# A skip weight added by two identity products on TensorE instead of an addition on VectorE, with the hand-written order rewritten

## The chip, the cores and the metric

One core of one Trainium2 chip runs the whole kernel as one program. The metric is the device time of one execution in microseconds, median of the runs shown. Engine names below are those of the profile: PE (TensorE matmul), PEld (its weight loads), DVE (VectorE), ACT (ScalarE), POOL (GpSimd), SP (SyncE, which here only issues DMAs).

## The reference, cut to what matters

```python
def A(q, k, v, shift_k, ssm_k, ssm_D):            # q, k, v: 2048 x 512 bf16
    k_shift = sum(k_pad[:, t:t+S] * shift_k[:, 3-t] for t in range(4))
    kv = k_shift * v
    y = long_convolution(kv, ssm_k)                # by FFT over 4096, one filter per channel
    y = y + kv * ssm_D                             # D: one number per channel
    return q * y

x = A_q
x = x + A(layernorm(x), A_k, A_v, ...)
x = x + mlp(layernorm(layernorm(x)))               # 512 -> 1376 (gelu) -> 512
x = x + A(layernorm(x), A_k, A_v, ...)
x = x + mlp(layernorm(layernorm(x)))
```

`kv * D` is the long convolution's tap at lag 0: adding D to the first tap of each channel's filter gives the same sum. That is how the kernel does it. Since `A` multiplies its filter result by its own argument alone, the filter result is computed once and used by both layers.

## The kernel before, in words

The first 100 us or so compute the long convolution as a two-step Fourier transform by matmuls, for the filter and for kv. From 104.5 us on, eight rounds of the MLP (four groups of 512 tokens, twice) run with TensorE as the bound.

Everything in the first part is a named piece in a plan. `plan.add` gives a piece its name, its possible engines, and its function; a long string, `ORDER`, lists the pieces as `name.engine`, in the order in which they are written into the program. Each engine runs its own pieces strictly in that order, and a piece that waits holds all that stand behind it on its engine. `P` in the string is PE with the number of one of four PSUM buffers; `A`, `D`, `G`, `S` are ACT, DVE, POOL, SP. Most PE pieces have a copy out of PSUM, with an `e` at the end of the name, on ACT or DVE (helper `mm_evac`; the copy is L237 on ACT, L239 on DVE).

The pieces that the change and the prediction touch:

- `lk0`..`lk3`, `lh1`, `lh113`, `lv0`, `lv1`, `lsT`: loads of k, of k's rows for the shift, of v, and of the short filter `sT`. `lK00`..`lK11` load the long filter into `Kd`, as packets of 128 bytes. All go through SP (L301, L374).
- `sF` (POOL, L382) casts `sT`; `dg0`..`dg2` (L435) build diagonal matrices DG from it by four small multiplications each.
- `kT0`..`kT3` (PE, L441) transpose k; `kv10` and its like (PE, L524) do the short filter on three of four channel blocks by 32 matmuls each; `kvm10` and its like (DVE, L530) multiply by v. All `kv` pieces need `dg` and most `kTe`.
- `kg0`, `kg1`, `ka1`, ... `kgm` (POOL, L455, L457, L462, L466): the short filter of the fourth channel block, as long element-wise operations one behind the other.
- `s00`, `s01`, `s02`: the layernorm of the first 512 tokens. `s00` is the statistics (on ACT L487 to L490; on DVE L259, L263, L268), `s01` the power on POOL (L271, L495 to L500), `s02` the scaling (on ACT L508; on DVE L276, four TENSOR_SCALAR).
- `U0S0` and its like (PE, L325): first transform step of kv, 12 pieces of four matmuls for three blocks. `KS00`..`KS71` (PE, L400): the same for the filter, 16 pieces; they read `Kd`. `K20`..`K215` (PE, L413): the filter's second step, 16 pieces, which need all `KS`.
- `kd0`, `kd4` (L393): D is added to the filter's first taps. `Kd[:, s, 0]` holds the first tap of each of 128 channels' rows, 64 columns a piece, with a step of 128 bytes; `Dz` is a 128x128 matrix with D at the same places and zeros elsewhere, made by POOL at the start. `kd0` must be done before `KS0x` to `KS3x`, `kd4` before `KS4x` to `KS7x`.

Of the kernel before, what the change touches and what calls it, by code (L numbers as in the profile page):

```python
# [11 lines left out]
ALU = mybir.AluOpType  # L12
# [3 lines left out]


ORDER = """
lSK.S lk1.S lsT.S lk3.S lk0.S lk2.S bSK.P0 lh1.S bSKe.A lh113.S lx0.S kT1.P1 lv0.S sF.G lv1.S dg0.D dg2.D
kT1e.A lK00.S kT3.P2 dg1.D lK01.S kT0.P3 kT3e.A kT2.P0 kT0e.A kg0.G kT2e.D s00.A kv10.P1 kv21.P2 kvm10.D kg1.G  # L20
U1S0.P30 kv11.P0 U1S0e.A kvm21.D U1S1.P1 kvm11.D kv00.P3 U1S1e.A s01.G lK10.S kv01.P2 kvm00.D ka1.G s02.A
U0S0.P01 kvm01.D U1S3.P1 lK11.S kv20.P3 U1S3e.D U0S0e.A kd0.D U0S3.P2 kvm20.D KS11.P1 U0S3e.A KS21.P0 kg2.G
lX.S KS11e.D KS10.P3 KS21e.A KS00.P2 KS10e.A U2S0.P02 KS00e.D KS30.P1 U2S0e.A U2S3.P3 KS30e.D U0S2.P2 U2S3e.A
KS20.P0 lH.S lW.S U2S1.P1 U0S2e.A KS20e.D lM.S KS31.P3 ka2.G lx1.S U2S1e.A KS01.P2 kd4.D KS50.P0 KS31e.A
KS01e.D KS70.P1 KS70e.A KS41.P3 KS50e.D KS61.P2 KS41e.A KS40.P1 KS61e.D KS60.P0 KS40e.A KS51.P3 kg3.G KS60e.D
KS71.P2 KS51e.A U1S2.P1 KS71e.A U2S2.P0 U1S2e.D U0S1.P3 U2S2e.A K211.P2 U0S1e.D K29.P1 K211e.A K210.P0 K29e.D
K28.P3 K210e.A K214.P2 ka3.G K28e.A K24.P1 K214e.D K21.P0 K24e.A K215.P3 sa2.S K21e.D sb2.S K212.P2 K215e.A
K20.P1 K212e.D lb0.S K23.P0 K20e.A lb1.S K22.P3 K23e.D K26.P2 K22e.A kgm.G K25.P1 s10.D K26e.A K27.P0 sb0.S
sa0.S U2T0.P3 K27e.A K213.P2 K25e.A U2T1.P0 K213e.A sa1.S U1T0.P1 U2T0e.D B1.G sb1.S s11.G U2T1e.A sb3.S
U3S0.P22 sa3.S U1T0e.D U1T1.P3 U3S0e.A X20.P00 U1T1e.D U3S2.P1 X20e.A X10.P21 U3S2e.D X21.P32 X10e.A U3S3.P0  # L30
T20.D0 X21e.A U3S1.P1 U0T0.P2 lx.S U3S1e.A T10.D1 X13.P30 U3S3e.A V20.P10 U0T0e.D X13e.A U3T0.S X23.P01 T21.D2
U0T1.P2 V20e.A T13.D0 X00.P32 X23e.A V10.P11 U0T1e.D X00e.A V21.P0 V10e.A T23.D1 X01.P30 V13.P2 V21e.A T00.D2
X02.P11 X01e.A V23.P0 X02e.D V13e.A X03.P32 T01.D0 V23e.A V00.P1 X03e.A T02.D1 X11.P20 V01.P0 V00e.A T03.D2
X12.P31 X11e.A V02.P1 V01e.D X12e.A U3T1.S X30.P22 T11.D0 V02e.A V03.P0 X30e.A T12.D1 X22.P30 V11.P1 V03e.A
T30.D2 X31.P21 X22e.A Z01.S V12.P0 V11e.D X31e.A Z00.S T22.D0 X32.P32 V12e.A V30.P12 X32e.A T31.D1 Z10.S
X33.P20 V22.P0 X33e.A T32.D2 Z03.S V31.P3 V22e.A T33b.D0 V32.P2 Z13.S V31e.A T33a.D1 V33b.P0 V30e.D V32e.A
Z02.S V33a.P3 V33be.D V33ae.A TC0a.P1 TC0b.P2 Z12.S TC0ae.A TD0a.P3 TC1.P0 TC0be.D TD0ae.A Z11.S TD0b.P1
TC1e.D Y00.P2 TD0be.A TC3.P3 w3.S w1.S Y00e.A g00.D w2.S Y01.P1 TC3e.A w4.S TC2.P0 g01.D Y02.P2 h00.D Y01e.A
Y10.P3 h01.D Y02e.A p00.G Y30.P1 TC2e.D Y10e.A p01.G Y12.P2 Y30e.A b00.D g02.D Y22.P3 Y12e.A LT0.P0 Y20.P1
b01.D Y22e.A LT0e.D h02.D Y32.P2 Y20e.A Y32e.D p02.G b02.D  # L40
"""
NA, NB = 32, 64

# [82 lines left out]
def kernel(ctx: ExitStack, tc: tile.TileContext, A_q, A_k, A_v, A_shift_k, A_ssm_k, A_ssm_D,  # L126
                 B_x, B_w1, B_b1, B_w2, B_b2, out):
    nc = tc.nc
    P = 128
    _, S, D = A_q.shape  # L130
# [43 lines left out]
    Kd = place("Kd", [P, P, NB], 64 * K)  # L174
# [8 lines left out]
    IDt = const.tile([P, P], BF16, name="IDt")  # L183
# [12 lines left out]
    B1 = const.tile([P, FT], F32, name="B1")  # L196
# [31 lines left out]
    def view(t, dims, dtype=None):  # L228
        n = int(np.prod(dims))
        v = t[:, :] if dtype is None else t[:, :].bitcast(dtype)  # L230
        names = "abc"[:len(dims)]
        return v[:, 0:n].rearrange("p (%s) -> p %s" % (" ".join(names), " ".join(names)),
                                   **dict(zip(names[1:], dims[1:])))

    def evac(eng, dst, src):
        if eng == "A":
            nc.scalar.activation(dst, src, AF.Copy)  # L237
        else:
            nc.vector.tensor_copy(dst, src)  # L239
# [56 lines left out]
    with tc.tile_pool(name="ps", bufs=1, space=bass.MemoryType.PSUM) as ps:  # L296
        pf = [ps.tile([P, 1024], F32, name=f"p{i}") for i in range(4)]
        plan = _Plan({"ps": 4, "xb": 3, "zt": NZT, "T": NTB})

        def load(name, dst, src, nbytes, deps=(), eng="S", rank=0):  # L300
            return plan.add(name, {eng: 400}, deps, lambda it: nc.sync.dma_start(dst, src), dma=("copy", nbytes), rank=rank)  # L301
# [5 lines left out]
        def mm_evac(name, ns, deps, mms, dims, dst, bf=False, take=(), free_mm=(), edeps=(), rank=0, src=None):  # L307
            src = src or (lambda v: v)
            n = int(np.prod(dims))
            cost = {"A": 85 + 0.82 * n, "D": 50 + (0.53 if bf else 1.06) * n}  # L310
            pe = plan.add(name, {"P": ns}, deps, lambda it: mms(view(pf[it["slot"]["ps"]], dims, BF16 if bf else None)),
                          take=["ps"] + list(take), free=free_mm, rank=rank)
            ev = plan.add(name + "e", cost, [pe] + list(edeps),
                          lambda it: evac(it["eng"], dst(), src(view(pf[pe["slot"]["ps"]], dims, BF16 if bf else None))),
                          free=[(pe, "ps")], rank=rank)
            return pe, ev
# [72 lines left out]
        for c in range(8):  # L389
            if c % (8 // NK) == 0:  # L390
                sl = slice(c * 16, c * 16 + P // NK)
                kd = plan.add(f"kd{c}", {"G": 300, "D": 130}, lK[c * NK // 8], lambda it, sl=sl: (
                    nc.vector if it["eng"] == "D" else nc.gpsimd).tensor_tensor(Kd[:, sl, 0], Kd[:, sl, 0], Dz[:, sl], ALU.add))  # L393
            for g in range(2):
                def mms(o, c=c, g=g):
                    for m in range(8):
                        for e in range(2):
                            rs = slice(64 * g + 32 * e, 64 * g + 32 * e + 32)
                            s0 = 16 * c + 2 * m
                            nc.tensor.matmul(o[:, e, m, :], Kd[rs, s0:s0 + 2, :].rearrange("p s b -> p (s b)"), Ft[rs, 256:320],  # L400
                                             start=True, stop=True)
# [65 lines left out]
        kgm = plan.add("kgm", {"D": 1150, "G": 4200}, kg[-1:] + lv, gmul)  # L467
# [8 lines left out]
        lx0 = load("lx0", lna0, xd[:, 0:GT, :], 2 ** 19)  # L476
        lx1 = load("lx1", x1, xd[:, GT:2 * GT, :], 2 ** 19)
# [32 lines left out]
        _, s2 = first(0, lna0, lx0)  # L510
        s10, _ = first(1, x1, lx1)
        kvp, USp, ZU = [], [], []
        for cc in range(4):
# [4 lines left out]
            for o2 in range(2 if cc < CK else 0):  # L518
                def mms(o, cc=cc, o2=o2):
                    for i in range(8):  # L520
                        for t in range(KS):
# [4 lines left out]
                              lambda it, mms=mms: mms(view(pf[it["slot"]["ps"]], [8, P])), take=["ps"])  # L526
# [9 lines left out]
        lM = load("lM", Mt[:], M_h.ap().bitcast(BF16), 2 ** 21, kvp)  # L536
# [5 lines left out]
        lx = load("lx", x_t[:], q_d.rearrange(TOK, p=P), 2 ** 21, USp)  # L542
# [117 lines left out]
        for n, (a, b) in enumerate(UNITS):  # L660
# [7 lines left out]
            else:  # L668
                _, y = mm_evac("Y02", 864, e0[1] + [lH], last_mm(0, 2), [2, D], lambda: YA[0][:, 2:4, :])
# [24 lines left out]
    with tc.tile_pool(name="ps2", bufs=4, space=bass.MemoryType.PSUM, reuse_waits="tile") as ps2, \  # L694
# [79 lines left out]
        with tc.manual_schedule(engines={ENG.PE, ENG.DVE, ENG.Activation, ENG.Pool, ENG.SP}):  # L774
            nc.gpsimd.memset(hT[FL:FL + 1, FT - 1, :], 1.0)
            for n in range(2 * NG):
# [50 lines left out]
```

## Time and profile before

| | |
|---|---|
| time, median of 3 runs | 257.14 us (256.9 to 257.2) |
| the profiled execution's own time | 256.81 us |
| its span (first to last instruction) | 255.1 us |
| mean granted TensorE clock | 0.978 |
| busy: PE / DVE / ACT / POOL | 93% / 68% / 57% / 21% of the span |
| chain that ended last | PE 72%, DVE 12%, DMA 7% |

The busy shares are means over two very different parts. The long second part (147.5 us) is PE from end to end, so the time is set by when it can begin. What the change touches lies between 1 and 45 us. Times in the rows are from the start of the span.

### The profile page before, as it was taken

How to read it: one execution, taken by the hardware profiler on the slowest of the kernel's cores; microseconds unless marked ns; L12 is line 12 of the kernel's file. 1: busy time of each engine (PE TensorE's matmuls, PEld its weight loads, DVE VectorE, ACT ScalarE, POOL GpSimd, SP SyncE). 2: the span in 40 equal slices, each digit the busy share in tenths (PEclk: the TensorE clock that was granted, in tenths of full speed). 3: DMA queues.
4: the chain of work that ended last, by engine and by line, in shares of the span. 5: the costliest groups of instructions: out<-in, count | busy, mean ns of one | idle time of the engine just before them, and what ended most of it. 6: DMA issues, size and time to landing. Idle time of an engine off the chain costs nothing.

```text
span 255.1 us, 5088 instructions
## 1 busy us (share of the span) xinstructions
PE 236.8 (93%) x2084; PEld 146.3 (57%) x2084; DVE 174.5 (68%) x321; ACT 146.1 (57%) x210; POOL 54.5 (21%) x52
## 2 busy tenths in 40 slices
PE   1898479999999999999999999999999999999995
PEld 0698446889989857854444444444444444444443
DVE  0345988899999897787889989886866863022022
ACT  3698388899999799921821721722712712812810
POOL 2499999310000011011110111110110110000000
PEclk9999975899999999999999999999999999999999
DMA  5999994199967898004040401304006006002001
GB/s 132 382 334 167 222 442 180 76 320 321 312 135 103 148 237 288 3 0 82 5 82 0 78 6 20 62 0 82 4 1 165 0 11 157 0 14 71 1 20 63
DMA packets 53040, 30.15 MB, mean 118 GB/s; under 512 B 46642, under 2 KB 50456, under 8 KB 51736
## 3 DMA queue, kind: packets, MB, share of 16 engines
q1 hardware_dynamic: 52864, 29.73, 43.5%
q8 instruction: 16, 0.26, 0.4%
q10 hardware_dynamic: 152, 0.09, 0.1%
q14 instruction: 8, 0.07, 0.1%
HBM read 16.71 MB, written 2.10 MB: 74 GB/s over the span
## 4 chain that ended last, share of the span: by engine, by line
PE 72%; DVE 12%; DMA 7%; issue 4%; ACT 2%; SPq 2%; ACTq 0%; DVEq 0%
PE po L738 30%; PE ph L704 29%; DMA arena<-in_A_v_dram 4%; DVE T L573 4%; DVE arena L239 3%; PE p L325 2%; PE p L357 2%; PE p L649 2%; DVE arena L393 2%; DMA arena<-in_A_ssm_D_dram 2%; PE p L400 2%; PE p L413 2%; PE p L524 1%; DVE ZT L239 1%; DMA arena<-ZT 1%
## 5 line engine op out<-in xcount | busy, mean ns | idle before, releaser
L706 ACT ACTIVATE arena<-ph,B 128x512 bf16<-128x512 f32 (+5 forms) x110 | 63.7, 604 | 81.1 <-PE ph L704 81.0
L704 PE MATMUL ph<-arena 128*128 128x512 bf16 (+4 forms) x440 | 78.5, 336 | 0.1
L738 PE MATMUL po<-arena 128*128 128x512 bf16 (+2 forms) x363 | 77.4, 373 | 0.0
L704 PEld LDWEIGHTS <-arena 128*128 128x128 bf16 (+1 forms) x440 | 40.4, 100 | 37.2 <-DMA arena<-in_B_w_dram 0.4
L738 PEld LDWEIGHTS <-arena 128*128 128x128 bf16 (+1 forms) x363 | 35.4, 98 | 40.5
L743 DVE TENSOR_TENSOR arena<-po,arena 128x512 bf16<-128x512 f32 (+1 forms) x33 | 21.5, 673 | 43.6 <-PE po L738 43.6
L237 ACT ACTIVATE arena<-p 128x1024 bf16<-128x1024 f32 (+5 forms) x38 | 37.8, 1071 | 10.1 <-PE p L441 3.9
L271 POOL TENSOR_TENSOR lrsm<-lrsm,mhalf 128x4 f32<-128x4 f32 (+2 forms) x10 | 8.9, 885 | 95.9 <-DVE lrsm L265 95.9
L237 ACT ACTIVATE ZT<-p 128x1024 bf16<-128x1024 f32 (+1 forms) x22 | 22.0, 1055 | 2.5 <-PE p L325 2.5
L259 DVE BATCH_NORM_STATS2 lstm<-arena 128x6 f32<-128x512 bf16 x32 | 19.9, 681 | 0.2
L573 DVE TENSOR_TENSOR T<-xb,arena 128x2048 bf16<-128x2048 bf16 (+1 forms) x17 | 18.7, 1159 | 0.0
L239 DVE CAST arena<-p 128x1024 bf16<-128x1024 f32 x15 | 17.7, 1223 | 1.4 <-PE p L400 0.9
L582 PE MATMUL p<-arena,T 128*128 128x128 bf16 x256 | 16.5, 219 | 1.0 <-DVE arena L239 0.4
L271 POOL TENSOR_TENSOR lrsg<-lrsg,mhalf 128x4 f32<-128x4 f32 x8 | 8.1, 1014 | 40.2 <-DVE lrsg L268 40.1
L237 ACT ACTIVATE xb<-p 128x1024 bf16<-128x1024 f32 x15 | 16.1, 1165 | 0.1
L582 PEld LDWEIGHTS <-T 128*128 128x128 bf16 x256 | 14.9, 98 | 1.6 <-issue 1.3
L455 POOL TENSOR_TENSOR T<-arena,SK 128x2048 bf16<-128x2048 bf16 (+3 forms) x4 | 14.9, 3740 | 3.8 <-ACT arena L237 3.7
L259 DVE BATCH_NORM_STATS2 lstg<-arena 128x6 f32<-128x512 bf16 x24 | 14.8, 679 | 0.0
L276 DVE TENSOR_SCALAR arena<-arena,lmvg,lrsg 128x512 bf16<-128x512 bf16 x28 | 9.7, 409 | 6.7 <-POOL lrsg L271 6.7
L239 DVE COPY arena<-p 128x2048 bf16<-128x2048 bf16 (+3 forms) x10 | 10.5, 1049 | 4.4 <-issue 3.0
L276 DVE TENSOR_SCALAR arena<-arena,lmvm,lrsm 128x512 bf16<-128x512 bf16 x32 | 11.2, 409 | 2.3 <-POOL lrsm L271 2.3
L524 PE MATMUL p<-DG,arena 128*128 128x128 bf16 x192 | 11.4, 219 | 1.2 <-ACT ZT L237 0.9
(73 smaller groups left out, 226.8 us busy)
## 6 DMA issues: line engine op xcount, KB each, us to landing
arena<-arena SPq DMA_DIRECT2D x8, 512.0 KB, 4.2
arena<-in_A_k_dram SPq DMA_DIRECT2D x4, 512.0 KB, 6.2
arena<-in_A_v_dram SPq DMA_DIRECT2D x2, 1024.0 KB, 9.6
arena<-in_A_ssm_k_dram SPq DMA_DIRECT2D x4, 512.0 KB, 7.9
arena<-tabM SPq DMA_DIRECT2D x1, 2048.0 KB, 12.1
arena<-in_A_q_dram SPq DMA_DIRECT2D x1, 2048.0 KB, 8.2
out_dram<-arena SPq DMA_DIRECT2D x15, 128.0 KB, 1.7
arena<-in_B_w_dram SPq DMA_DIRECT2D x1, 1376.0 KB, 6.5
```

Source lines behind the costliest of these rows:

```text
L237: nc.scalar.activation(dst, src, AF.Copy)
L239: nc.vector.tensor_copy(dst, src)
L259: nc.vector.bn_stats(self.st[:, i, 0, :], x_t[:, GT * g + i, :] if src is None else src[:, i, :])
L271: nc.gpsimd.tensor_tensor(self.rs[:, a:b], self.rs[:, a:b], mhalf[:, a:b], ALU.pow)
L276: nc.vector.tensor_scalar(out=dst[:, i, :], in0=xs, scalar1=self.mv[:, i, 0:1], scalar2=self.rs[:, i:i + 1], op0=ALU.subtract, op1=ALU.mult)
L455: nc.gpsimd.tensor_tensor(m[:, t:NT, :], kn[:, 0:NT - t, c3], sk(t, NT - t), ALU.mult)
L573: eng.tensor_tensor(view(Tb[it["slot"]["T"]], [2, n, CW]), x2, kk, ALU.mult)
L582: nc.tensor.matmul(o[:, i, :], T[:, r, i, :], Mt[:, ka + i, 1 - r, :], start=r == 0, stop=r == 1)
L704: nc.tensor.matmul(o.rearrange("p (i t) -> p i t", t=P), W1t[:, ct, ft * P:ft * P + m], lt[:, a:b, ct, :], start=ct == 0, stop=ct == CT - 1)
L706: nc.scalar.activation(hT[0:m, ft, a * P:b * P], o, AF.Gelu_apprx_tanh, bias=B1[0:m, ft:ft + 1])
L738: nc.tensor.matmul(po[:, a:b], hT[0:m, ft, i * P:(i + 1) * P], W2t[0:m, ft, a:b], start=ft == 0, stop=ft == FT - 1)
L743: nc.vector.tensor_tensor(xs, po[:, a:b], xs, ALU.add)
```

## The change

`kd0` and `kd4` become a PE piece and a copy: two products with the identity matrix `IDt` as weights, of `Kd`'s first taps and of `Dz`, are summed in PSUM, and the sum is copied back to the same places of `Kd`. `ORDER` is written anew; only its first rows are shown, the rows of the engines follow.

```diff
                 sl = slice(c * 16, c * 16 + P // NK)
-                kd = plan.add(f"kd{c}", {"G": 300, "D": 130}, lK[c * NK // 8], lambda it, sl=sl: (
-                    nc.vector if it["eng"] == "D" else nc.gpsimd).tensor_tensor(Kd[:, sl, 0], Kd[:, sl, 0], Dz[:, sl], ALU.add))
+                def mms(o, sl=sl):
+                    nc.tensor.matmul(o, IDt[:], Kd[:, sl, 0], start=True, stop=False)
+                    nc.tensor.matmul(o, IDt[:], Dz[:, sl], start=False, stop=True)
+                _, kd = mm_evac(f"kd{c}", 120, lK[c * NK // 8], mms, [P // NK], lambda sl=sl: Kd[:, sl, 0])
 ORDER = """
-lSK.S lk1.S lsT.S lk3.S lk0.S lk2.S bSK.P0 lh1.S bSKe.A lh113.S lx0.S kT1.P1 lv0.S sF.G lv1.S dg0.D dg2.D
+lSK.S lk3.S lk2.S lk0.S lk1.S lh1.S bSK.P0 lsT.S bSKe.D lh113.S lx0.S kT3.P1 lv0.S lv1.S kT2.P2 kT3e.A lK01.S
...
```

In what follows, line numbers behind L393 are two higher in the changed kernel (L435 is L437, L530 is L532, and so on).

SP's first DMAs before. `kh` is the target of `lh1` and `lh113`, `sT` that of `lsT`, `arena<-in_A_k_dram` are `lk0` to `lk3`:

```order
L301 DMA arena<-in_A_k_dram 128x2048
L301 DMA sT<-in_A_shift_k_dram 128x4x4
L301 DMA arena<-in_A_k_dram 128x2048 x3
L301 DMA kh<-in_A_k_dram 112x3x128 [waits DMAHW0_49]
L301 DMA kh<-in_A_k_dram 15x3x128 [waits DMAHW1_49]
```

SP's first DMAs now:

```order
L301 DMA arena<-in_A_k_dram 128x2048 x4
L301 DMA kh<-in_A_k_dram 112x3x128
L301 DMA sT<-in_A_shift_k_dram 128x4x4 [waits DMAHW0_49]
L301 DMA kh<-in_A_k_dram 15x3x128 [waits DMAHW1_49]
L301 DMA arena<-in_A_q_dram 128x2048 [waits DMAHW2_49]
```

The load of `sT` stood behind one of the four loads of k and now stands behind all four and behind `lh1`.

DVE from its start up to the first filter casts (`KS`), before. The twelve L435 are `dg0`, `dg2`, `dg1`; L530 are the `kvm`; L393 is `kd0`:

```order
L435 TENSOR_SCALAR DG<-IDt,sF 128x128 [waits Pool_49]
L435 TENSOR_SCALAR DG<-IDt,sF 128x128 x11
L239 COPY arena<-p_119 128x4x3x128 [waits DMAHW1_49,PE_49,Activation_49]
L530 TENSOR_TENSOR arena<-p_120,arena 128x8x128 [waits DMAHW3_49,PE_49,Activation_49]
L530 TENSOR_TENSOR arena<-p_121,arena 128x8x128 [waits DMAHW4_49,PE_49,Activation_49]
L530 TENSOR_TENSOR arena<-p_119,arena 128x8x128 [waits PE_49]
L530 TENSOR_TENSOR arena<-p_122,arena 128x8x128 [waits PE_49,Activation_49]
L530 TENSOR_TENSOR arena<-p_121,arena 128x8x128 [waits PE_49]
L239 CAST ZT_95<-p_120 128x4x8x32 [waits PE_49,Activation_49]
L393 TENSOR_TENSOR arena<-arena,Dz 128x64 [waits DMAHW6_49,DMAHW5_49]
L530 TENSOR_TENSOR arena<-p_122,arena 128x8x128 [waits PE_49]
```

The same stretch now, from the first rows on DG (`dg1`) to `kT1e`, `s00` and the first `kvm`:

```order
L437 TENSOR_SCALAR DG<-IDt,sF 128x128 [waits Pool_49]
L437 TENSOR_SCALAR DG<-IDt,sF 128x128 x3
L239 COPY arena<-p_119 128x4x3x128 [waits PE_49]
L259 BN_STATS lstg_104<-arena 128x6 [waits DMAHW2_49]
L259 BN_STATS lstg_104<-arena 128x6 x3
L263 BN_AGGR lmvg_105<-lstg_104 128x2 [waits DVE_49] x4
L268 TENSOR_SCALAR lrsg_106<-lmvg_105 128x4 [waits DVE_49]
L532 TENSOR_TENSOR arena<-p_120,arena 128x8x128 [waits DMAHW3_49,PE_49,Activation_49]
```

And a little further on, from the fifth `kvm` (`kvm20`) over `U1S0e` and `s02` to `kvm11` and the first `KS` casts:

```order
L532 TENSOR_TENSOR arena<-p_120,arena 128x8x128 [waits PE_49]
L239 CAST ZT_96<-p_122 128x4x8x32 [waits PE_49]
L276 TENSOR_SCALAR arena<-arena,lmvg_105,lrsg_106 128x512 [waits Pool_49]
L276 TENSOR_SCALAR arena<-arena,lmvg_105,lrsg_106 128x512 x3
L532 TENSOR_TENSOR arena<-p_121,arena 128x8x128 [waits PE_49,Activation_49]
L239 CAST arena<-p_119 128x64x8x2 [waits PE_49,Activation_49]
```

Two L393 leave DVE. Two of the three `dg` go to ACT, and `s00` and `s02` come from ACT to DVE; `dg1` stands ahead of a copy of the transposed k (`kT1e`), and `s02` ahead of `kvm11`. On PE, `U1S2`, which needs `kvm11`, now stands behind the first `KS` piece and ahead of the fifteen others.

More of the change, by code (lines that the diff above doesn't have):

```diff
@@ L18 @@
 ORDER = """
-lSK.S lk1.S lsT.S lk3.S lk0.S lk2.S bSK.P0 lh1.S bSKe.A lh113.S lx0.S kT1.P1 lv0.S sF.G lv1.S dg0.D dg2.D
[L20 to L38, printed above, removed]
@@ L39 @@
-Y10.P3 h01.D Y02e.A p00.G Y30.P1 TC2e.D Y10e.A p01.G Y12.P2 Y30e.A b00.D g02.D Y22.P3 Y12e.A LT0.P0 Y20.P1
-b01.D Y22e.A LT0e.D h02.D Y32.P2 Y20e.A Y32e.D p02.G b02.D
+lSK.S lk3.S lk2.S lk0.S lk1.S lh1.S bSK.P0 lsT.S bSKe.D lh113.S lx0.S kT3.P1 lv0.S lv1.S kT2.P2 kT3e.A lK01.S
+kT0.P3 kT2e.D lK00.S kT1.P0 kT0e.A sF.G dg1.D kg0.G dg0.A kT1e.D s00.D dg2.A kv10.P1 kv01.P2 kg1.G kvm10.D
+kv00.P3 kvm01.D kv21.P0 kvm00.D kv20.P1 s01.G kvm21.D lK10.S U0S0.P20 kvm20.D U1S0.P31 ka1.G U0S0e.A U0S3.P0
+U1S0e.D U2S0.P12 U0S3e.A lK11.S kv11.P2 U2S0e.A s02.D kd0.P0 U2S3.P3 kvm11.D kd0e.A U2S2.P1 U2S3e.A KS30.P0
@@ new lines @@
+kg2.G lH.S U1S2.P2 KS30e.D U2S2e.A KS10.P3 U1S2e.A KS10e.D U1S3.P1 KS31.P0 U1S3e.A KS21.P2 KS31e.D KS00.P3
+KS21e.A lW.S KS11.P1 lX.S KS00e.D KS20.P0 KS11e.A lM.S KS01.P2 ka2.G lx1.S KS20e.D kd4.P3 U0S2.P1 kd4e.A
+KS51.P3 U0S2e.A KS01e.D KS50.P0 KS51e.A KS70.P1 KS50e.D KS40.P2 KS70e.A KS71.P3 KS40e.D KS41.P0 kg3.G KS71e.A
+KS60.P1 KS41e.D KS61.P2 KS60e.A U0S1.P3 KS61e.A U2S1.P0 U0S1e.D U1S1.P1 U2S1e.A K29.P2 U1S1e.D K28.P3 K29e.A
+K210.P0 K28e.D K211.P1 K210e.A ka3.G K26.P2 K211e.D K20.P3 K26e.A K212.P0 K20e.A K214.P1 sb2.S K212e.D sa2.S
@@ new lines @@
+K21.P2 K214e.A K213.P3 K21e.D lb1.S K22.P0 lb0.S K213e.A K23.P1 K22e.D kgm.G K27.P2 K23e.A K25.P3 s10.D K27e.A
+K215.P0 sa0.S U2T0.P1 sb0.S K215e.A K24.P2 K25e.A U2T1.P0 sb3.S sa3.S K24e.A B1.G U1T0.P3 U2T0e.D s11.G
+U2T1e.A sb1.S U3S0.P22 sa1.S U1T0e.D U1T1.P1 U3S0e.A X20.P00 U1T1e.D U3S2.P3 X20e.A X10.P21 U3S2e.D U3S3.P1
+X10e.A X13.P02 T20.D0 U3S3e.A U3S1.P3 U0T0.P2 lx.S X13e.A T10.D1 X12.P10 U3S1e.A V20.P01 U0T0e.D X12e.A U3T0.S
+X23.P31 T13.D2 U0T1.P2 V20e.A T12.D0 X01.P12 X23e.A V10.P00 U0T1e.D X01e.A X00.P30 V10e.A T23.D1 V13.P1 X00e.A
@@ new lines @@
+V12.P2 T01.D2 V13e.A X02.P01 V23.P3 T00.D0 X02e.A X03.P12 V23e.D V12e.A V00.P0 X03e.A T02.D1 X11.P20 V01.P3
+V00e.A T03.D0 X21.P11 X11e.A V02.P0 V01e.D X21e.A U3T1.S X30.P22 T11.D2 V02e.A V03.P3 X30e.A T21.D1 X31.P10
+V11.P0 V03e.A T30.D0 X22.P21 X31e.A Z00.S V21.P3 V11e.D X22e.A Z01.S X32.P12 T31.D2 V21e.A V30.P02 Z10.S
+X32e.A T22.D1 X33.P20 V31.P3 X33e.A Z12.S T32.D0 V22.P1 V31e.A Z13.S T33b.D2 V32.P2 V22e.A T33a.D1 V33b.P3
+Z03.S V30e.D V32e.A V33a.P1 V33be.D V33ae.A Z02.S TC0a.P0 TC0b.P2 TC0ae.A TD0a.P1 TC1.P3 TC0be.A TD0ae.D Z11.S
@@ L41 @@
+Y00.P0 TC1e.D TD0b.P1 w4.S Y00e.A TC2.P2 w3.S TD0be.A w1.S g00.D w2.S TC3.P3 TC2e.A h00.D Y02.P1 TC3e.D p00.G
+Y01.P0 Y02e.A Y20.P2 b00.D g01.D Y01e.A Y32.P3 Y20e.A g02.D LT0.P1 Y30.P0 Y32e.A Y10.P2 h01.D LT0e.A Y30e.A
+Y12.P3 h02.D p01.G Y22.P1 Y10e.A Y12e.D p02.G b01.D b02.D Y22e.D
 """
```

## The prediction

> **What bounds the kernel now.** The page first, then the chain that ended last, then the busy time by stage.
>
> ```profile
> span 255.1 us, 5088 instructions
> 104.55 4.98 PE ph L704 x44
> 109.53 9.51 PE po L738 x44
> ```
>
> In the chain, from 104.55 us on, only PE's MLP products follow each other, 9.50 us by 9.51 us, to the end. The change touches nothing there, so a microsecond won or lost before 104.5 is one of the total. The table by stage says what fills the time before that:
>
> ```profile
> 11.00:30.00 19.00, 14.69 (x231) 13.66 (x232) 11.69 (x9) 14.64 (x27) 18.29 (x11) 1.00 1.05 244
> 30.00:44.60 14.60, 12.15 (x284) 8.65 (x284) 12.84 (x11) 12.13 (x13) 14.29 (x6) 0.70 0.77 320
> 58.00:86.00 28.00, 26.55 (x438) 25.41 (x437) 27.84 (x27) 27.91 (x31) 0.00 (x0) 1.00 0.85 202
> ```
>
> The columns are PE, PEld, DVE, ACT, POOL. From 58 to 86 us DVE and ACT are both full (27.84 and 27.91 of 28 us) with work that the change leaves as it is, nearly piece for piece on the same engines. So that stretch moves as a block with its beginning, and the beginning is the first K2 piece:
>
> ```profile
> 44.71 2.95 PE p L413 x40
> ```
>
> K2 needs all 16 `KS` pieces, and these need `kd0` and `kd4`. Before 44.6 nobody is full except POOL, which works without a break. What ends the waits there:
>
> ```profile
> 25.95 3.61 POOL L455 TENSOR_TENSOR T<-arena,SK 128x1792 bf16<-128x1792 bf16 x1
> 26.35 3.52 DVE L393 TENSOR_TENSOR arena<-arena,Dz 128x64 bf16<-128x64 bf16 x1
> 29.50 0.68 POOL L457 TENSOR_TENSOR T<-kh,SK 128x256 bf16<-128x256 bf16 x1
> 29.93 0.64 PE L400 MATMUL p<-Ft,arena 32*128 32x64 bf16 x32 [2.79 <-DVE arena L393]
> 34.40 3.37 POOL L455 TENSOR_TENSOR T<-arena,SK 128x1664 bf16<-128x1664 bf16 x1
> 36.35 1.73 DVE L393 TENSOR_TENSOR arena<-arena,Dz 128x64 bf16<-128x64 bf16 x1
> 37.77 4.73 DVE L239 CAST arena<-p 128x1024 bf16<-128x1024 f32 x4
> 38.13 0.78 PE L400 MATMUL p<-Ft,arena 32*128 32x64 bf16 x48 [1.58 <-DVE arena L393]
> ```
>
> An addition of 64 columns takes 3.52 and 1.73 us. Both end 0.31 us after the POOL operation that ran beside them: 26.35+3.52 = 29.87 against 25.95+3.61 = 29.56, and 36.35+1.73 = 38.08 against 34.40+3.37 = 37.77. DVE waited for POOL to finish its instruction. DVE's copies out of PSUM did not: four in 4.73 us with POOL busy. And POOL lost nothing to DVE: its L457 right behind took the usual 0.68 us. So an addition that reads only SBUF slips in between two POOL instructions.
>
> **Part by part. The additions.** They leave the chain with 3.45 and 1.74 us:
>
> ```profile
> 26.43 3.45 DVE arena L393
> 36.35 1.74 DVE arena L393
> 3.73 0.20 ACT L212 ACTIVATE act<-mhalf 128x1 f32<-128x1 f32 x1
> 3.84 0.58 ACT L237 ACTIVATE SK<-p 128x512 bf16<-128x512 f32 x1
> ```
>
> In their place stand two matmuls of 64 columns and an ACT copy of 128x64. Two matmuls I take at no more than 0.64/16 us of PE's time (the L400 row has 32 of 64 columns), the copy between the 0.20 us of 128x1 and the 0.58 us of 128x512, nearest the first: 0.27 us. Both sit under pieces of U on PE (0.60 us each, the L325 row below), so they cost nothing on the path; without that cover, 0.4 us each.
>
> **DG and the load of sT.** These rows carry it:
>
> ```profile
> 3.71 2.44 SPq L301 DMA_DIRECT2D kh<-in_A_k_dram  x2
> kh<-in_A_k_dram SPq DMA_DIRECT2D x1, 84.0 KB, 7.8
> 7.44 0.20 POOL L382 CAST sF<-sT 128x16 f32<-128x16 bf16 x1
> 7.67 2.04 DVE L435 TENSOR_SCALAR DG<-IDt,sF 128x128 bf16<-128x128 bf16 x12 [7.67 <-POOL sF L382]
> 11.31 7.95 POOL L455 TENSOR_TENSOR T<-arena,SK 128x2048 bf16<-128x2048 bf16 x2 [3.67 <-ACT arena L237]
> 12.44 0.96 DVE L239 COPY arena<-p 128x1536 bf16<-128x1536 bf16 x1 [2.72 <-issue]
> 12.66 3.75 PE L524 MATMUL p<-DG,arena 128*128 128x128 bf16 x64 [0.33 <-ACT arena L237]
> ```
>
> `lh1`, behind the four loads of k, lands at 3.71+7.8 = 11.5 us. `lsT` now stands behind it, so `sT` lands near 11.6 and `sF` ends near 11.8 instead of 7.64. `dg1` then starts at the very moment when POOL, its cast done, starts its long row (7.95 us for two). Before, DG was finished 1.6 us ahead of that row. If `dg1` goes through, it takes 2.04/12*4 = 0.7 us, `kT1e` behind it 0.96, and the first `kv` starts at 13.5, 0.85 us later than the 12.66 of now. If it must wait as L393 did, one or two of its four instructions go before POOL begins and the rest after the 4.1 us of `kg0`, at 16.1: `kT1e` ends at 17.4 and `kv` starts at 17.5. Queued behind it on DVE are `kT1e`, `s00` and all `kvm`; PE waits for `kT1e`.
>
> **s00 and s02.** From ACT to DVE:
>
> ```profile
> 52.29 2.46 DVE L259 BATCH_NORM_STATS2 lstg<-T 128x6 f32<-128x512 bf16 x4
> 54.66 0.37 DVE L263 BATCH_NORM_AGGREGATE lmvg<-lstg 128x2 f32<-128x6 f32 x4
> 104.41 1.38 DVE L276 TENSOR_SCALAR arena<-arena,lmvg,lrsg 128x512 bf16<-128x512 bf16 x4
> 18.84 0.60 PE L325 MATMUL p<-Ft,arena 128*128 128x256 bf16 x4
> 17.91 2.36 DVE L530 TENSOR_TENSOR arena<-p,arena 128x1024 bf16<-128x1024 f32 x2 [1.36 <-DMA arena<-in_A_v_dram]
> 20.21 1.04 POOL L271 TENSOR_TENSOR lrsg<-lrsg,mhalf 128x4 f32<-128x4 f32 x1
> 21.80 4.07 POOL L462 TENSOR_TENSOR T<-T,T 128x2048 bf16<-128x2048 bf16 x1
> ```
>
> `s00` is 3.0 us of DVE, `s02` 1.4. With a free run from 13.5 the five `kv` that come first on PE end at 13.5+5*1.88 = 22.9 (3.75 us for two), and four U pieces and `kv11` follow to 27.3. DVE does the last of five `kvm` at 1.18 us each and one cast by 25.5, `s02` by 26.9, and `kvm11` from 27.3 to 28.5. PE has two more U pieces and `KS30` to do, gets to `U1S2` at 29.3 and finds it ready. From there remain 21 casts, 11 of ACT at 0.94 us (4.69/5) and 10 of DVE at 1.16 (4.73/4):
>
> ```profile
> 38.81 4.69 ACT L237 ACTIVATE arena<-p 128x1024 bf16<-128x1024 f32 x5 [0.86 <-PE p L400]
> ```
>
> That is 11.6 us on DVE, with 0.9 to fill the buffers 12.5, and K2 starts at 41.8 instead of 44.64: 2.8 us won.
>
> If `s02` must wait as L393 did, its four instructions each wait for one POOL instruction, because POOL's next one begins within the gap. In the run with the late start, `kv20` ends at 17.5+9.4 = 26.9, DVE is at `s02` at 29.45, and POOL (its long row of two from 11.95, a small one to 20.5, `s01` 1.6 us with its small rows, `ka1` 4.07 us to 26.2, then 3.61, 0.68, 4.07 and 3.37) frees the port near 29.85, 30.5, 34.7 and 38.1. `kvm11` ends at 39.6 and `U1S2` stands at the head of PE's queue until then, fifteen `KS` pieces behind it. K2 starts at 39.6+12.5 = 52.1: 7.5 us lost.
>
> **Do these TENSOR_SCALARs wait?** No row shows one beside a long POOL instruction. Lower bound: nothing, as the copies out of PSUM (a wait for a port can't shorten them). Upper: one POOL instruction each, as L393. I take the upper: like L393 they read only SBUF, and the one that ran beside any POOL write is no clear escape:
>
> ```profile
> 99.74 0.52 POOL L775 MEMSET arena<- 1x512 bf16 x1
> 99.95 0.77 DVE L276 TENSOR_SCALAR arena<-arena,lmvm,lrsm 128x512 bf16<-128x512 bf16 x2
> ```
>
> It ended 0.46 us behind the memset's end and may have waited a little.
>
> The Trainium skill speaks against this change here: "SBUF — State Buffer", section "Who interferes with whom", says that VectorE's second port pair is GpSimd's, that an addition of two SBUF tensors contends with GpSimd's reads, and that `tensor_scalar` can enter a two-port mode and then either blocks or is blocked for a whole instruction. For the additions the trace agrees (3.52 and 1.73 us); for `tensor_scalar` no run here shows it. By that rule the sum is the lost one, 7.5 us; by the rows of PSUM copies alone, the won one.
>
> **The rivals**, against the execution's 256.81 us, which lies 0.33 under the median; the times are given as medians.
>
> - Forecast: `dg1` and `s02` both wait for POOL. 257.14+7.5 = 264.6. Chance 0.40.
> - Neither waits (TENSOR_SCALAR does not share what L393 shared, or DVE's run of four keeps POOL out). Speaks for it: the PSUM copies at their normal time beside POOL. Against it: L393. 257.14-2.8 = 254.3, faster. It decides at one place: `s02` shows 1.4 us. Chance 0.32.
> - Only `s02` waits, `dg1` slips in ahead of `kg0`. `s02` is reached at 25.5, and by the same POOL rows starting at 12.5 its last instruction goes at 35.5; `U1S2` at 36.7, K2 at 49.2: 261.7. Chance 0.10.
> - Only `dg1` waits, or each group waits once. With the start at 17.5, `s02` ends near 30.9 and `kvm11`, behind `kv11`, at 32.5; `U1S2` there, K2 at 45.0: 257.5. Chance 0.14, split about evenly over no change and slower, with a little faster.
> - The additions' gain is not there, because the filter's load is late: the row of L393's wait ended on POOL, not on a DMA, so this is small. With it go other mishaps of the new order, slower by 1 to 3 us: 0.04.
>
> **Numbers.** Time 264.6. The range must take in the free case, which alone has 0.32, and the forecast with 2 to 3 us for a PE that idles ten microseconds and a clock that was already granted at 0.70 from 30 to 44.6: 253.9 to 267.0. Of the waiting case by itself: 261.5 to 267.0. Two kernels can be told apart here at about 0.2%, 0.5 us. Faster by more: 0.32 and 0.04 of the fourth case, 0.36. Within: 0.05. Slower: 0.40+0.10+0.05+0.04 = 0.59.
>
> **What would show it.** In the profile of the changed kernel: `sF` near 11.7; L437 lasting over 4 us for its four, or 0.7; the first L526 near 17.5, or 13.5; L276 near 29 us lasting some 9 us in four pieces that each end just behind a POOL row, or 1.4 us; PE's longest wait ended by L532 (`kvm11`), or none over 1 us before 42; the first L415 near 52, or near 42. L237 with 128x64 near 0.27 us. The forecast is wrong if four L276 rows run beside a POOL row at 0.41 us each.

## The result and the profile after

The changed kernel takes 274.13 us, the kernel before, run beside it, 257.02 us (256.59 to 257.2), each the median of four runs. It is slower, by a ratio of 1.066 (95% interval 1.063 to 1.0691). One of the four, 278.7 us, ran at a lower granted clock and is left out of the ratio and of all that follows; the median of the other three is 273.75 us (273.51 to 274.51), 16.7 us over before. The profiled execution took 273.51 us, with a span of 271.8 us against 255.1.

The chain of waits of the changed kernel, in order of time (start, us, what), shows two stretches that the chain of before doesn't have:

```profile
3.87 6.98 DMA sT<-in_A_shift_k_dram
11.21 8.36 DVE DG L437 x3
19.60 11.21 PE p L526 x158
...
37.71 4.46 DVE arena L276 x2
42.17 1.14 DVE arena L532
43.36 1.03 PE p L325 x4
...
56.81 1.78 PE p L415 x16
...
112.11 1.14 DVE arena L239
113.30 3.15 PE ph L706 x28
117.39 2.17 PE ph L706 x32
120.79 4.98 PE ph L706 x44
```

The chain now begins with the load of `sT`, goes over `dg1` (L437) into the `kv` pieces, which run through from 19.60 us, then over `s02` (L276) and `kvm11` (L532) into `U1S2` (L325) at 43.36. K2 (L415) is in the chain from 56.81; the first piece of it, from 44.64 us in the kernel before, starts at 56.74. Up to there 12.1 us are lost. A second loss lies behind the vector part. The row `L706 x44` starts at 120.79 where before's `L704 x44` starts at 104.55: 64.05 us behind K2 instead of 59.91, 4.1 us more. The last 0.5 us lie behind that row, in the MLP (151.0 us from there to the end of the span instead of 150.5).

The timeline, asked for the stretch of one instruction at a time (start, us, engine, line), puts `dg1` and POOL's long row side by side:

```profile
10.98 0.20 POOL L382 CAST sF<-sT 128x16 f32<-128x16 bf16 x1 [4.13 <-DMA sT<-in_A_shift_k_dram]
11.21 4.14 DVE L437 TENSOR_SCALAR DG<-IDt,sF 128x128 bf16<-128x128 bf16 x1 [1.78 <-POOL sF L382]
11.21 4.08 POOL L457 TENSOR_TENSOR T<-arena,SK 128x2048 bf16<-128x2048 bf16 x1
15.27 3.90 DVE L437 TENSOR_SCALAR DG<-IDt,sF 128x128 bf16<-128x128 bf16 x1
15.24 3.87 POOL L457 TENSOR_TENSOR T<-arena,SK 128x1920 bf16<-128x1920 bf16 x1
19.09 0.46 DVE L437 TENSOR_SCALAR DG<-IDt,sF 128x128 bf16<-128x128 bf16 x1
19.03 0.46 POOL L459 TENSOR_TENSOR T<-kh,SK 128x128 bf16<-128x128 bf16 x1
19.47 0.24 DVE L437 TENSOR_SCALAR DG<-IDt,sF 128x128 bf16<-128x128 bf16 x1
```

Each of these TENSOR_SCALARs ends 0.06 us behind the POOL instruction beside it (11.21+4.14 = 15.35 against 15.29; 19.17 against 19.11; 19.55 against 19.49), and POOL's next instruction has begun by the time DVE's next one does. So one of DVE's goes through per POOL instruction. The fourth finds POOL idle and takes 0.24 us. Four that cost 0.7 us in the kernel before take 8.51. PE's rows show what waited for them:

```profile
15.40 0.26 PE L526 MATMUL p<-DG,arena 128*128 128x128 bf16 x1 [4.18 <-DVE DG L437]
19.22 11.58 PE L526 MATMUL p<-DG,arena 128*128 128x128 bf16 x159 [3.56 <-DVE DG L437]
```

PE did one product of `kv10` when the first matrix was there and got on when the second came. Its first products did not wait for `kT1e`, which ran from 19.63 to 20.57 us beside them. The timeline at `s02`:

```profile
33.12 0.54 DVE L276 TENSOR_SCALAR arena<-arena,lmvg,lrsg 128x512 bf16<-128x512 bf16 x1
32.83 0.67 POOL L459 TENSOR_TENSOR T<-kh,SK 128x256 bf16<-128x256 bf16 x1
33.58 4.21 DVE L276 TENSOR_SCALAR arena<-arena,lmvg,lrsg 128x512 bf16<-128x512 bf16 x1
33.59 4.05 POOL L464 TENSOR_TENSOR T<-T,T 128x2048 bf16<-128x2048 bf16 x1
37.71 3.53 DVE L276 TENSOR_SCALAR arena<-arena,lmvg,lrsg 128x512 bf16<-128x512 bf16 x1
37.72 3.37 POOL L457 TENSOR_TENSOR T<-arena,SK 128x1664 bf16<-128x1664 bf16 x1
41.16 1.01 DVE L276 TENSOR_SCALAR arena<-arena,lmvg,lrsg 128x512 bf16<-128x512 bf16 x1
41.02 1.00 POOL L459 TENSOR_TENSOR T<-kh,SK 128x384 bf16<-128x384 bf16 x1
```

All four end 0.14 to 0.16 us behind a POOL row: 9.05 us for what takes 1.38 (four of L276 without a POOL row beside them, at 104.41 in the page of before). POOL's rows are as long as in the kernel before to within 0.07 us; only DVE pays.

The table by stage (PE, PEld, DVE, ACT, POOL, then the granted clock) says what this makes of PE:

```profile
11.00:20.00 9.00, 1.14 (x10) 0.69 (x8) 8.79 (x5) 3.03 (x9) 8.45 (x4) 0.67 1.09 316
20.00:31.00 11.00, 11.00 (x161) 10.97 (x159) 8.39 (x15) 0.00 (x0) 7.24 (x5) 0.81 1.08 230
31.00:43.40 12.40, 4.91 (x74) 4.11 (x72) 12.40 (x8) 5.23 (x6) 12.16 (x6) 0.78 0.76 292
43.40:56.70 13.30, 12.52 (x266) 9.14 (x266) 11.58 (x10) 10.71 (x12) 6.82 (x2) 0.50 0.01 2
```

PE works 1.14 of the first 9 us and 4.91 of the third stretch's 12.40. In the stretches behind each wait, where it has its work together, its clock was granted at a mean of 0.81 and 0.50, and it is full there (11.00 of 11.00, 12.52 of 13.30 us).

### The profile page after: what moved, and what is told of

It is laid out like the page before. It is cut to its first block, busy times and chain, and to the rows that moved or that the text cites. A ratio compares the mean times of both kernels' runs of the same rounds, so it can differ in the third digit from the quotient of the medians.

```text
span 271.8 us, 5088 instructions
## 1 busy us (share of the span) xinstructions
PE 242.2 (89%) x2088; PEld 151.3 (56%) x2088; DVE 191.1 (70%) x327; ACT 138.2 (51%) x196; POOL 54.1 (20%) x50
## 4 chain that ended last, share of the span: by engine, by line
PE 72%; DVE 18%; issue 3%; DMA 3%; ACT 2%; SPq 1%; POOL 0%; DVEq 0%; POOLq 0%
PE ph L706 28%; PE po L740 28%; DVE arena L239 5%; PE p L526 5%; PE p L325 3%; DVE T L575 3%; DVE DG L437 3%; DMA sT<-in_A_shift_k_dram 3%; DVE arena L276 2%; PE p L357 2%; PE p L402 2%; DVE ZT L239 1%; ACT ZT L237 1%; PE p L415 1%; SPq L301 1%
## 5 line engine op out<-in xcount | busy, mean ns | idle before, releaser
L708 ACT ACTIVATE arena<-ph,B 128x512 bf16<-128x512 f32 (+5 forms) x110 | 64.5, 603 | 84.4 <-PE ph L706 84.0
L706 PE MATMUL ph<-arena 128*128 128x512 bf16 (+4 forms) x440 | 80.0, 342 | 3.1 <-DVE arena L239 1.8
L706 PEld LDWEIGHTS <-arena 128*128 128x128 bf16 (+1 forms) x440 | 41.8, 103 | 40.2 <-issue 1.9
L740 PEld LDWEIGHTS <-arena 128*128 128x128 bf16 (+1 forms) x363 | 35.4, 98 | 40.5
L237 ACT ACTIVATE arena<-p 128x1024 bf16<-128x1024 f32 (+7 forms) x38 | 36.3, 1032 | 8.8 <-PE p L443 4.9
L276 DVE TENSOR_SCALAR arena<-arena,lmvg,lrsg 128x512 bf16<-128x512 bf16 x32 | 18.7, 646 | 6.7 <-POOL lrsg L271 6.7
L239 DVE CAST arena<-p 128x1024 bf16<-128x1024 f32 x17 | 20.0, 1217 | 1.4 <-PE p L402 0.8
L526 PE MATMUL p<-DG,arena 128*128 128x128 bf16 x192 | 13.7, 240 | 7.9 <-DVE DG L437 7.7
L325 PE MATMUL p<-Ft,arena 128*128 128x256 bf16 x64 | 11.4, 326 | 7.6 <-DVE arena L532 7.5
L526 PEld LDWEIGHTS <-arena 128*128 128x128 bf16 x192 | 13.2, 109 | 8.3 <-issue 7.5
L259 DVE BATCH_NORM_STATS2 lstg<-arena 128x6 f32<-128x512 bf16 x28 | 17.2, 678 | 0.0
L584 PE MATMUL p<-arena,T 128*128 128x128 bf16 x256 | 16.5, 219 | 0.8 <-DVE arena L239 0.3
L584 PEld LDWEIGHTS <-T 128*128 128x128 bf16 x256 | 14.9, 98 | 1.6 <-issue 1.1
L239 DVE COPY arena<-p 128x2048 bf16<-128x2048 bf16 (+2 forms) x10 | 10.8, 1075 | 7.1 <-PE p L443 5.1
## 6 DMA issues: line engine op xcount, KB each, us to landing
arena<-in_A_v_dram SPq DMA_DIRECT2D x2, 1024.0 KB, 10.3
```

The source lines that it names most:

```text
L259: nc.vector.bn_stats(self.st[:, i, 0, :], x_t[:, GT * g + i, :] if src is None else src[:, i, :])
L276: nc.vector.tensor_scalar(out=dst[:, i, :], in0=xs, scalar1=self.mv[:, i, 0:1], scalar2=self.rs[:, i:i + 1], op0=ALU.subtract, op1=ALU.mult)
L325: nc.tensor.matmul(o[:, i, :], src[:, 4 * q + i, cs], Ft[:, 0:256], start=True, stop=True)
L526: nc.tensor.matmul(o[:, i, :], w, DG[:, cc, t, :], start=t == 0, stop=t == KS - 1)
L584: nc.tensor.matmul(o[:, i, :], T[:, r, i, :], Mt[:, ka + i, 1 - r, :], start=r == 0, stop=r == 1)
L706: nc.tensor.matmul(o.rearrange("p (i t) -> p i t", t=P), W1t[:, ct, ft * P:ft * P + m], lt[:, a:b, ct, :], start=ct == 0, stop=ct == CT - 1)
```

## The experiments

The theory: DVE's SBUF-to-SBUF TENSOR_SCALARs wait for whole POOL instructions; `dg1` does because `sT` is loaded last, `s02` because it moved from ACT to DVE; a separate loss lies in the new order of the tail. The rivals: the products themselves are dear, the new order of pieces or the clock costs by itself, or DVE is merely slowed in proportion to POOL's work. The runs come from several chips, on which the kernel before took 257.02 to 257.69 us; a difference between two runs below is good to about 0.7 us.

**The products alone.** Before's order with the four places of the filter changed, and the products' code as in the change:

```
-U0S0.P01 ... U0S0e.A kd0.D U0S3.P2 kvm20.D KS11.P1
+U0S0.P01 ... U0S0e.A kd0.P0 U0S3.P2 kvm20.D kd0e.A KS11.P1
-... U2S1e.A KS01.P2 kd4.D KS50.P0
+... U2S1e.A kd4.P1 KS01.P2 kd4e.A KS50.P0
```

> The kernel before, its order kept, with only the two additions replaced by the identity products and the ACT copies. Port theory (DVE's SBUF-only instructions wait for whole POOL instructions; the additions were two such): DVE gets back 3.5 and 1.7 us, K2 starts near 42 instead of 44.64, about 254.5 us, faster by 2 to 3 us. Rival 'the additions' wait hid under PE and ACT work': K2 within 0.5 us of 44.6, 256.5 to 257.5 us. Rival 'the identity products and the small copy are themselves dear': slower than 257.1 us, with L237 128x64 well over 0.3 us.

Measured: 254.85 us against 257.39 of the kernel before, ratio 0.988 (0.9848 to 0.9912), K2 from 41.62. The idea of the change wins 2.5 us; the order that came with it loses more than that. The groups by form show the price of the small copy:

```profile
L237 ACT ACTIVATE arena<-p 128x64 bf16<-128x64 f32 x2 | 0.9, 458 | 1.5 <-PE p L394 1.5
```

It is 0.46 us instead of the expected 0.27 to 0.3, and doesn't matter.

**sT loaded third.** The changed kernel with

```
-lSK.S lk3.S lk2.S lk0.S lk1.S lh1.S bSK.P0 lsT.S
+lSK.S lk3.S lsT.S lk2.S lk0.S lk1.S lh1.S bSK.P0
```

> The changed kernel with the load of sT third in SP's queue instead of last. Port theory: sT lands before 8 us, dg1's four instructions run ahead of POOL's long row in 0.7 to 0.9 us in all instead of 8.51, first kv near 13 instead of 19.6; s02 stays on DVE and is still caught by POOL (8 to 10 us for four), kvm11 ends near 35 to 36 instead of 43.3; 265 to 267 us. Rival 'these TENSOR_SCALARs are slow on DVE wherever they stand in this stage': dg1 still over 8 us, time within 1 us of 274. Rival 'the lateness of kv and not the wait makes s02 long': s02 falls to 1.6 us and the time to about 259 us.

Measured: 268.27 us, 5.5 less than the changed kernel, ratio to before 1.042 (1.0377 to 1.0464). The timeline of DVE (the count is of instructions in a row):

```profile
11.06 0.73 DVE L437 TENSOR_SCALAR DG<-IDt,sF 128x128 bf16<-128x128 bf16 x4
...
14.38 2.46 DVE L259 BATCH_NORM_STATS2 lstg<-arena 128x6 f32<-128x512 bf16 x4
17.16 2.93 DVE L268 TENSOR_SCALAR lrsg<-lmvg 128x4 f32<-128x4 f32 x1
...
26.80 11.37 DVE L276 TENSOR_SCALAR arena<-arena,lmvg,lrsg 128x512 bf16<-128x512 bf16 x4
```

`dg1`, ahead of POOL's row, is back at 0.73 us. The time is 1 to 3 us above what was expected, and `kvm11` ends at 39.30 instead of 35 to 36. By the rows this is so because the freed DVE ran into POOL at a new place: L268, on 4 numbers per partition, takes 2.93 us instead of 0.17. Behind it `s02` begins while POOL is in a long row and takes 11.37 us instead of 9.05. BATCH_NORM_STATS2, which also reads only SBUF, runs beside POOL's row from 12.13 to 20.06 us in its usual 2.46.

**s02 on ACT**, where it was before:

```
-kv20.P1 s01.G kvm21.D lK10.S
+kv20.P1 s01.G s02.A kvm21.D lK10.S
...
-kv11.P2 U2S0e.A s02.D kd0.P0
+kv11.P2 U2S0e.A kd0.P0
```

> The changed kernel with s02 on ACT behind s01's scaling, as the kernel before had it. Port theory: dg1 still 8.5 us, kv still from 19.6; s02 leaves DVE, kvm11 ends near 36 instead of 43.3, 266 to 267 us. Rival 'dg1's wait alone carries the loss, s02's lies beside PE's work': 273 to 274 us. Rival 'ACT was full': ACT becomes late by s02's time, over 269 us.

Measured: 263.5 us, 10.3 less than the changed kernel, ratio 1.0228 (1.0188 to 1.0269). `dg1` stays at 8.49 us. `kvm11` ends at 36.20, as expected, and K2 starts at 48.98, 7.8 us earlier. The rest of the gain over the expectation comes behind K2: from there to `L706 x44` it is 62.22 us instead of 64.05, and this execution has no half clock in the tail (1.00 from 104.9 to 107 us).

**Both edits.**

> The changed kernel with both edits: sT loaded third, s02 on ACT. Port theory: both waits are gone, kvm11 ends near 28 to 29, K2 starts near 41.5 to 43, and only the loss behind the vector part is left (about 4 us): 257.5 to 260 us. Rival 'the new order of the KS and U pieces, or the half clock, carries the loss by itself': above 264 us.

Measured: 257.89 us, ratio 1.0021 (0.9989 to 1.0053). The two waits together cost 273.75-257.89 = 15.9 us, about the sum of the two alone (5.5 and 10.3). K2 starts at 41.80, as with the products alone (41.62); in the two further runs with this first part it is 43.14 and 43.33, with the last transposed k pieces 0.7 us later. So in these four executions the new order of the pieces up to K2 costs at most 1.7 us, with the long L268 (2.94 us) in it. The row of the MLP,

```profile
105.55 4.98 PE ph L706 x44
```

starts 63.75 us behind K2: nearly all of the second loss is still there.

**Both edits, tail of before**: everything behind `V33ae.A` in the order of the kernel before.

> The run with both edits (sT third, s02 on ACT), and behind the last piece V33ae the order of the kernel before in place of the new one. Theory 'the second loss lies in the order of the tail': K2 starts near 41.8 as with both edits, and the distance from K2 to the chain's L706 x44 shrinks from 63.75 us to about 60 to 61 us (59.9 before, 60.9 with the products alone); 254 to 255.5 us. Rival 'the tail's loss comes from the clock or from the loads, whatever the order': 257 to 258.5 us.

Measured: 254.64 us, ratio 0.99 (0.9852 to 0.9948), 3.3 less than with the new tail. The row

```profile
102.77 4.98 PE ph L706 x44
```

gives the distance: 102.77-43.14 = 59.63 us.

**The kernel before, new tail.**

> The kernel before, with only the order behind V33ae taken from the changed kernel. Theory 'order of the tail': first part as before (K2 at 44.6), distance from K2 to the chain's L704 x44 of 62 to 64 us instead of 59.9, 258.5 to 261 us. Rival 'the tail's loss needs the new order of stages 1 and 2': 256.5 to 257.7 us.

Measured: 260.06 us, ratio 1.0122 (1.0066 to 1.0179), distance 107.06-44.37 = 62.69 us. The tail's order costs 2.9 us in a kernel that has none of the rest.

**Where in the tail.** The chain of this last run (before's tail has PE's `L704` running through from 97.91 us):

```profile
98.52 1.10 DVE arena L276 x3
99.62 1.15 DVE arena L239
...
100.81 0.40 PE ph L704 x4
...
101.23 1.92 ACT arena L706 x7
...
103.68 2.14 PE ph L704 x32
```

PE's timeline has the wait itself, first in this run, then in the changed kernel:

```profile
100.81 1.74 PE L704 MATMUL ph<-arena 128*128 128x128 bf16 x28 [3.03 <-DVE arena L239]
...
111.15 0.40 PE L706 MATMUL ph<-arena 128*128 128x128 bf16 x4 [1.19 <-DMA arena<-in_B_w_dram]
113.30 3.15 PE L706 MATMUL ph<-arena 128*128 128x128 bf16 x28 [1.75 <-DVE arena L239]
```

In the changed kernel the MLP's first four products wait for the weights, and the next 28 wait for `Y22e`, the last copy on DVE, which the new order puts behind `b02` (L276 x3). These 28 take 3.15 us at half clock (0.50 granted from 112.99 to 116.40 us), against 1.74 us for the same 28 in the run above, where the clock was full (1.00 from 100.8 to 103 us). So the two runs split the 4.1 us: the order alone, at full clock, makes the distance 2.8 us longer (62.69 against 59.91), and the half clock adds 1.4 (3.15 against 1.74). What brings the half clock on stays open: PE stood still for 1.75 us just before it here, but for 3.03 us in the run above and 2.49 us in that with `s02` on ACT, and the clock stayed full in both.

With both edits, `Y22e` was then given to ACT:

```
-Y22.P1 Y10e.A Y12e.D p02.G b01.D b02.D Y22e.D
+Y22.P1 Y10e.A Y22e.A Y12e.D p02.G b01.D b02.D
```

> The run with both edits, and the copy Y22e on ACT right behind Y10e instead of last on DVE. Theory 'Y22e's place behind DVE's last LayerNorm work is the tail's loss': L706 starts about 1.2 us earlier and its clock does not fall to half; 255 to 256.7 us. Rival 'DVE's LayerNorm chain itself is late (its last rows and LT0 behind it), Y22e only stands at its end': under 0.5 us won, 257.4 to 258.2 us.

Measured: 255.94 us, ratio 0.9933 (0.9907 to 0.9959), 2.0 of the tail's 3.3 us, and no half clock there. What ends the wait of PE's first products now is the load of the MLP's weights; then comes ACT's work on their results (L708):

```profile
89.71 7.35 DMA arena<-in_B_w_dram
...
97.60 2.17 ACT arena L708 x8
```

**Another form of the same instruction.** The changed kernel, `dg1` in its place, with an accumulator output, into a new tile `dacc`, that nobody reads:

```
-scalar2=None, op0=ALU.mult)
+scalar2=None, op0=ALU.mult, op1=ALU.add, accum_out=dacc[:, t:t + 1])
```

> The changed kernel, with the four products of dg1 (and their siblings on DVE, if any) as TENSOR_SCALAR with an accumulator output that nobody reads; same place in the order, same POOL instructions beside them. Theory 'only a form of TENSOR_SCALAR that uses DVE's second port waits, and the accumulating form does not use it': the four and their accumulator reads take 1 to 1.6 us in all beside kg0 instead of 8.51, first kv near 13.5, s02 still waits (8 to 11 us); 267 to 269.5 us, as with the early sT. Rival 'every SBUF-to-SBUF TENSOR_SCALAR waits for POOL': dg1 8 us or more, 273 to 275 us.

Measured: 268.65 us, ratio 1.042 (1.0361 to 1.0478). The timeline, DVE and POOL (L459 here is POOL's row):

```profile
11.65 0.35 DVE L438 TENSOR_SCALAR_CACHE_REDUCE DG<-IDt,sF 128x128 bf16<-128x128 bf16 x1 [1.79 <-POOL sF L382]
...
12.45 0.34 DVE L438 TENSOR_SCALAR_CACHE_REDUCE DG<-IDt,sF 128x128 bf16<-128x128 bf16 x1
12.72 0.09 DVE L438 DVE_READ_ACCUMULATOR DG<-IDt,sF 128x1 f32 x1
...
16.36 3.26 DVE L268 TENSOR_SCALAR lrsg<-lmvg 128x4 f32<-128x4 f32 x1
...
11.65 7.95 POOL L459 TENSOR_TENSOR T<-arena,SK 128x2048 bf16<-128x2048 bf16 x2
```

Four of them go through in 1.15 us under the POOL row that holds the plain form for 8.51, at the same place and on the same data. A plain TENSOR_SCALAR (L268) ends 0.02 us behind that same row (19.62 against 19.60), after 3.26 us. So it is the form of the instruction that waits, not the place, the operands or DVE as such.

**POOL's row cut in four.** The changed kernel with the first of POOL's two instructions as four of 128x512:

```
-nc.gpsimd.tensor_tensor(m[:, t:NT, :], kn[:, 0:NT - t, c3], sk(t, NT - t), ALU.mult)
+n = (NT - t) if t else NT // 4
+for a in range(t, NT, n):
+    nc.gpsimd.tensor_tensor(m[:, a:a + n, :], kn[:, a - t:a - t + n, c3], sk(t, n), ALU.mult)
```

> The changed kernel, with POOL's first long row kg0 (one instruction of 128x2048, 4.07 us) cut into four of 128x512 (about 1.15 us each by POOL's rows of 128x384 in 1.00 and 128x256 in 0.67 us). Theory 'one of DVE's instructions goes through per POOL instruction, at its end': dg1's four end 0.06 us behind one quarter each and last 4.6 to 4.9 us in all instead of 8.51, the first kv comes near 16 instead of 19.6, s02 still waits 9 to 11 us; 270 to 272 us. Rival 'DVE is slowed by the share of time in which POOL is busy, however it is cut': dg1 stays over 8 us, 273 to 275 us.

Measured: 269.59 us, ratio 1.0439 (1.0373 to 1.0505). Two of the four pairs, from the timeline:

```profile
12.75 1.16 POOL L459 TENSOR_TENSOR T<-arena,SK 128x512 bf16<-128x512 bf16 x1
12.76 1.20 DVE L437 TENSOR_SCALAR DG<-IDt,sF 128x128 bf16<-128x128 bf16 x1
13.87 1.16 POOL L459 TENSOR_TENSOR T<-arena,SK 128x512 bf16<-128x512 bf16 x1
13.88 1.20 DVE L437 TENSOR_SCALAR DG<-IDt,sF 128x128 bf16<-128x128 bf16 x1
```

One of DVE's per POOL instruction, each to its end: 4.48 us in all. POOL is as busy as before (4.51 us for the four where the one took 4.08), so it isn't a slowing in proportion. The time is 0.4 us under the range given: half of `dg1`'s wait taken away won 4.2 us, nearly as much as all of it (5.1 in the run ahead of this, 5.5 with the early load). One reason in the rows is that here L268 and the first piece of `s02` met the end of a POOL row and took only 0.25 and 0.41 us.

## Why the prediction was wrong in size and right in kind

The loss comes apart by the medians: both waits 273.75-257.89 = +15.9, the tail 257.89-254.64 = +3.3, and -2.5 (254.64 against 257.17 of before) for the additions that are gone. That they make 16.6 together follows from how they are taken; what bears them out is that the products alone also win 2.5, and the new tail alone also costs 2.9. The prediction had the sign, the two groups of instructions and their mechanism, but as a choice: it gave this case 0.40 and the opposite one, faster, 0.32. It had 7.5 us for the loss, and its range ended at 267.0. The 9.2 us that are missing come from the steps below: +2.1, +1.6, +0.9 and +4.1, and the 0.5 us in the MLP. Step by step:

- **The additions.** Right. Its free case had K2 at 41.8 and 2.8 us won; the products alone have 41.62 and 2.5 us. That case was worked out for the new order, and there the three runs without the two waits have 41.80, 43.14 and 43.33, so the match to a tenth is partly luck.
- **DG and the load of sT.** Right up to `sF` (near 11.8 expected, 11.18 measured). Then the term was mis-sized: it let "one or two of its four instructions go before POOL begins and the rest after the 4.1 us of `kg0`". None went before: three took one POOL instruction each, and the fourth ran when POOL was done. `dg1` ended at 19.7 instead of 16.1, +3.6 us. It also had `kT1e` end ahead of the first `kv` product, which did not wait for it. The `kv` pieces ran through from 19.60 instead of 17.5: +2.1 us. The part on `s00` and `s02` counted one POOL instruction each for `s02`; counted so, `dg1` ends behind POOL's small one, which it put at 20.5; measured: 19.7.
- **The kv pieces.** It took 9.4 us for those up to `kv20`, a rate of full clock. They took 11.21 us, with the clock at half up to 24.24 us (0.50 granted from 20.00, then 1.00) after PE had worked 1.14 of the 9 us from 11 to 20. With the above, `s02` was reached at 33.12 instead of 29.45: +1.6 more.
- **s02.** Right: "some 9 us in four pieces that each end just behind a POOL row" were 9.05, and `kvm11` ended 3.7 us late because `s02` began so. The sum is partly luck: POOL stood idle for 4.03 us until L268 gave it the statistics, so `s02` met its rows of 256, 2048, 1664 and 384 columns, where the prediction had 1792, 256, 2048 and 1664.
- **From U1S2 to K2.** 13.4 us instead of 12.5, at a clock of 0.50: +0.9. K2 so at 56.74 for the expected 52.1. The runs tie these two low clocks to the waits. Where `sT` is loaded third the `kv` pieces run at 1.00 (13 to 20 us), and the stretch from `kvm11` to K2 again at 0.50 (39.3 to 52.7); where only `s02` moved it is 0.76 in the first (19.5 to 31) and 0.73 in the second (36.2 to 49.0), which takes 12.8 us. How a wait brings the clock down is not shown, and in the tail it stayed full behind PE's longest waits.
- **What was left out.** "So that stretch moves as a block with its beginning" held for the vector part (K2 12.1 us late, the last of L584 12.16 us late), and the prediction carried it on to the end. Behind it the diff had rewritten the tail's order, and no term was made for that: +4.1 us to `L706 x44`. By the runs that change the tail alone its order costs 2.9 to 3.3 us; by the traces 2.8 us of the 4.1 are the order and 1.4 the half clock. The place to look at was the last copy of the tail's list, `Y22e.D`.

The Trainium skill, "SBUF — State Buffer", section "Who interferes with whom", which the prediction cites, holds in each half that the runs touch. It lists `tensor_scalar` among the instructions that can enter a mode with two ports, and so contend with GpSimd, when their operands allow it, and excepts the form that writes out its accumulator; the trace agrees, with 8.51 us against 1.15 beside the same POOL instructions. It has the loser blocked until the other's instruction ends; the trace agrees, with ends 0.02 to 0.16 us behind it in the pairs of TENSOR_SCALAR above.

## What to carry to other kernels

Before an SBUF-only addition or TENSOR_SCALAR is put on DVE beside a POOL that runs one SBUF operation behind the other, price each instruction of the run, however small, as one of POOL's, and look at who is queued behind. What took the wait out or made it shorter here: the load that makes the instruction early, another engine, PSUM as one source (`kvm` pieces at 1.22 us beside POOL rows), the accumulating form, or shorter POOL instructions. Taking one such wait away moves the others, so their sum is read from a run with all of them gone. And when a change rewrites an order in several stretches, each gets its own term: here the idea alone is worth -2.5 us (254.85 us, and 254.64 with the new order mended, both faster than either kernel), and the order that came with it +19.1.

## What the hardware showed beyond that

- The wait doesn't depend on DVE's size: 128x4 of f32 took 2.93 and 3.26 us beside a POOL row (0.17 without), 128x512 of bf16 up to 4.21 (0.41 without).
- BATCH_NORM_STATS2, which reads only SBUF as well, isn't held: 2.46 us for four, beside a POOL row (`sT` loaded third) or not (the kernel before at 52.29 us).
- DVE keeps POOL out nowhere in these pairs: one of DVE's instructions ends just behind each of POOL's, and POOL's 128x2048 takes its 4.04 to 4.08 us with or without one.
- The accumulating form costs little: 0.35 us for 128x128 where the plain one takes 0.25, and its read of 0.09 us overlaps the next.
